# Half of a chunk's first product in Strassen's seven-product form, the second product in two PSUM banks, float16 in place of bfloat16

## The chip, the cores and the metric

One core of a Trainium2 chip. The metric is the device time of one execution, in microseconds (us). The kernel before takes 274.28 us (median of three runs, 274.2 to 274.58).

In the profile PE is TensorE's matmuls, PEld its weight loads, DVE is VectorE, ACT ScalarE, POOL GpSimd, SP SyncE.

## The reference, cut to what matters

```python
# q, k, v: 8 batches, 8 heads, 576 rows, 64 columns; w_in 512 x 2048, w_out 2048 x 512
q_s = softmax of q over its 64 columns;  k_s = softmax of k over its 576 rows
x   = q_s @ (k_s^T @ v)          # per head; put together: 4608 tokens x 512
h   = x @ w_in                   # the first product:  4608 x 512 x 2048
g   = h / (1 + exp(-h))          # Silu
out = g @ w_out                  # the second product: 4608 x 2048 x 512
```

The matmuls of `h` and `out` are nearly all the work. (The first three lines are shortened to words; the reference has them as numpy.)

## The kernel before

The tokens go in nine chunks of 512 (numbered 0 to 8; chunks 0 and 1 are special, the change concerns 2 to 8). While TensorE computes the first product of chunk t it also computes the second product of chunk t-1, in small units of four or eight matmuls (0.87 us each) that alternate. The second product is already in the seven-product (Strassen-Winograd) form: seven products of half-size blocks in place of eight, paid with sums of blocks (S1 to S4 of the activations, T1 to T4 of the weights) on VectorE.

A plain block of the first product is four matmuls into one PSUM bank, a tanh on ScalarE that reads the bank, and a "finishing product" on VectorE, `(tanh + 1) * h`, that reads the bank again. Only after it may the bank be written again. (`silu(h) = h/2 * (1 + tanh(h/2))`; tanh shares its table with exp: the trace has one table load in all.) Cuts are marked by dots, and the comments are added here.

```python
def silu(t, fb, i, o, w):                                   # i is the PSUM bank
    ...
    nc.scalar.activation(out=s, in_=i, func=ACT.Tanh, scale=OS)
    nc.vector.scalar_tensor_tensor(out=o, in0=s, scalar=1.0, in1=i, op0=ALU.add, op1=ALU.mult)

hb = [0, 2]                                                 # set to [2, 3] later: three banks rotate

def mm1(t, fb):
    bank = hb[0] % hb[1]
    hb[0] += 1
    mm1_mm(t, fb, bank, range(NC))                          # four matmuls of 512 columns
    mm1_silu(t, fb, bank)
...
WBANK = {1: 3, 6: 3, 7: 3, 4: 3, 5: 4, 3: 4, 2: 5}          # second product: three banks
...
for t in range(2, NCH):                                     # the order of units in a chunk
    begin[t] = len(units)
    bs = b_units(t - 1, ORDER)                              # 7 products x 2 halves of chunk t-1
    as_ = a_units(t)                                        # 16 plain blocks of chunk t
    plan(begin[t] + 2, lambda t=t: (s_op(t - 1, 1)))        # the sums S1 .. S4, on VectorE
    plan(begin[t] + 4, lambda t=t: (s_op(t - 1, 2)))
    plan(begin[t] + 10, lambda t=t: (s_op(t - 1, 3)))
    plan(begin[t] + 15, lambda t=t: (s_op(t - 1, 4)))
    ...                                                     # a, a, b, a, b, a, b ... one by one
...
for t in range(2, NCH - 1):                                 # attention work of batch b = t + 1
    ...                                                     # exp of q at units 4, 6; its row sums one unit later;
                                                            # exp of k at 9, 12; kv at 20; x of chunk t+1 at 25, 27
```

Each engine does its instructions in the order in which the program issues them; `plan(u, ...)` issues something just before unit u. The attention work in the last loop exists in chunks 2 to 6 (batches 3 to 7).

The softmax here doesn't subtract the row's maximum and nothing guards it: scores larger than these inputs give would overflow.

## Time and profile before

| | |
|---|---|
| time, span of the profiled run | 274.28 us, 272.5 us |
| TensorE busy | 263.6 us, 97% of the span |
| one chunk of the steady part (147.65 to 175.42 us) | 27.77 us: PE 27.56, DVE 22.16, ACT 17.31 |
| TensorE's clock | 1.00 throughout |

The page's first two parts, cut to TensorE. The rows of part 2 have one digit for each fortieth of the span: PE's busy tenths, and the clock that was granted, in tenths.

```profile
span 272.5 us, 5771 instructions
## 1 busy us (share of the span) xinstructions
PE 263.6 (97%) x2343; PEld 168.4 (62%) x2372; DVE 199.2 (73%) x290; ACT 158.2 (58%) x237; POOL 71.1 (26%) x62
## 2 busy tenths in 40 slices
PE   8999999999999999999999999999999999999993
...
PEclk9999999999999999999999999999999999999999
...
```

TensorE is the bound; nothing else is near it. The table of stretches for one chunk, us busy (with the number of instructions) for each engine, then the clock:

```profile
...
core 0: us, PE busy (x) PEld busy (x) DVE busy (x) ACT busy (x) POOL busy (x), PEclk, DMA share, GB/s
...
147.65:175.42 27.77, 27.56 (x261) 17.93 (x264) 22.16 (x31) 17.31 (x26) 7.42 (x4) 1.00 0.66 183
...
```

The longest waits of TensorE for a finishing product (engine, line, awaited; us in total, times, longest):

```profile
...
engine line waited for: us in total, times, longest us
...
PE PS L272 <- DVE GT L245: 0.3, 1, 0.3
...
```

0.3 us here, and two waits of 0.2 us in the special first chunks (another line): the three rotating banks absorb whatever VectorE is late. How late that is, the timeline of the same chunk shows (start, duration, instruction):

```profile
...
start us, us, engine line op out<-in xcount [idle before <-releaser]
...
150.08 1.03 PE L272 MATMUL PS<-XT,W 128*128 128x512 bf16 x4
...
151.15 0.60 ACT L244 ACTIVATE sg<-PS 128x512 f32<-128x512 f32 x1 [1.14 <-PE PS L272]
...
151.78 0.69 DVE L245 SCALAR_TENSOR_TENSOR GT<-sg,PS 128x512 f16<-128x512 f32 x1
...
158.38 2.29 DVE L335 TENSOR_TENSOR S<-GT 128x2048 f16<-128x2048 f16 x1
...
```

A block's matmuls run from 150.08 (ends are modelled; the next matmuls start at 150.95), its tanh starts at 151.15, its finishing product at 151.78, and its bank is free at 152.47. So an undisturbed block holds its bank for 1.5 us after its last matmul. S3 (158.38) takes 2.29 us beside GpSimd's work, where S1, a sum of the same size (at 150.64), took 1.22.

### The profile page before, as it was taken

The numbers are of one execution on the slowest core, as the hardware profiler recorded it, in microseconds if no ns is written. First come the engines' busy times: TensorE is split into PE (matmuls) and PEld (weight loads), VectorE is DVE, ScalarE is ACT, GpSimd is POOL, SyncE is SP. The second block draws the span as 40 slices with busy tenths as digits, with TensorE's granted clock in tenths as the row PEclk, the third lists the DMA queues.
The fourth block names the chain that finished last, engine by engine and source line by source line (L and its number), as shares of the span: only waits on it lengthen the run. The fifth ranks groups of instructions, "written<-read, shape, count | busy, mean of one in ns | idle before, by whom it ended". The sixth has DMA issues, their size and how long they took to land.

```text
span 272.5 us, 5771 instructions
## 1 busy us (share of the span) xinstructions
PE 263.6 (97%) x2343; PEld 168.4 (62%) x2372; DVE 199.2 (73%) x290; ACT 158.2 (58%) x237; POOL 71.1 (26%) x62
## 2 busy tenths in 40 slices
PE   8999999999999999999999999999999999999993
PEld 2467654445665566666666666666656665666783
DVE  2866765978998599749974998499837663877643
ACT  4767937667855585568546854685464446444410
POOL 1744970910470037002800180019000000000003
PEclk9999999999999999999999999999999999999999
DMA  7999999599886586648773968333134003300444
GB/s 251 321 198 352 254 339 329 169 291 377 272 169 236 112 259 144 250 98 241 170 259 81 242 176 264 81 77 67 23 69 88 2 0 77 79 0 0 95 101 116
DMA packets 35498, 45.85 MB, mean 168 GB/s; under 512 B 16208, under 2 KB 20048, under 8 KB 35472
## 3 DMA queue, kind: packets, MB, share of 16 engines
q1 hardware_dynamic: 29568, 33.69, 44.5%
q0 software_dynamic: 5584, 11.54, 16.3%
q8 instruction: 18, 0.29, 0.5%
q10 hardware_dynamic: 320, 0.26, 0.3%
q14 instruction: 8, 0.07, 0.1%
HBM read 36.70 MB, written 9.44 MB: 169 GB/s over the span
## 4 chain that ended last, share of the span: by engine, by line
PE 83%; DVE 8%; DMA 4%; ACT 2%; issue 1%; SPq 1%; POOL 1%; POOLq 0%
PE PS L272 36%; PE PS L361 33%; PE PS L301 5%; PE PS L252 4%; DMA vt<-in_v_dram 4%; DVE GT L245 2%; DVE S L335 2%; PE PS L222 2%; PE PS L183 2%; DVE zq L142 1%; SPq L95 1%; ACT sg L244 1%; DVE T L345 1%; DVE W L345 1%; POOL t L120 0%
## 5 line engine op out<-in xcount | busy, mean ns | idle before, releaser
L245 DVE SCALAR_TENSOR_TENSOR GT<-sg,PS 128x512 f16<-128x512 f32 (+2 forms) x144 | 96.3, 679 | 52.8 <-ACT sg L244 52.4
L244 ACT ACTIVATE sg<-PS 128x512 f32<-128x512 f32 (+2 forms) x144 | 85.8, 598 | 80.9 <-PE PS L272 74.1
L272 PE MATMUL PS<-XT,W 128*128 128x512 bf16 (+1 forms) x484 | 123.9, 375 | 1.8 <-DVE GT L245 0.3
L272 PEld LDWEIGHTS <-W 128*128 128x128 bf16 x512 | 49.8, 98 | 39.4 <-issue 2.1
L361 PEld LDWEIGHTS <-S 128*128 128x128 f16 x512 | 49.2, 98 | 16.6 <-issue 1.2
L151 POOL TENSOR_TENSOR eq<-eq,rzq 128x1152 bf16<-128x1152 bf16 x13 | 27.4, 2118 | 105.0 <-ACT sg L244 97.1
L361 PEld LDWEIGHTS <-GT 128*128 128x128 f16 x384 | 37.1, 98 | 13.1 <-issue 1.2
L361 PE MATMUL PS<-W,S 128*128 128x256 f16 x256 | 33.0, 273 | 0.1
L361 PE MATMUL PS<-W,GT 128*128 128x256 f16 x256 | 32.7, 273 | 0.1
L361 PE MATMUL PS<-T,S 128*128 128x256 f16 x256 | 32.7, 273 | 0.0
L335 DVE TENSOR_TENSOR S<-GT 128x2048 f16<-128x2048 f16 (+1 forms) x17 | 25.0, 1470 | 0.0
L585 POOL DMA_DIRECT2D out_dram<-ow x4 | 2.2, 552 | 75.7 <-DVE ow L570 75.7
L89 POOL CAST vaug<-vt 128x1152 bf16<-128x1152 f32 x12 | 20.4, 1732 | 0.0
L106 ACT ACTIVATE eq<-qt 128x1152 bf16<-128x1152 f32 x16 | 18.6, 1165 | 2.7 <-DMA qt<-in_q_dram 2.7
L109 ACT ACTIVATE ek<-kt 128x1152 bf16<-128x1152 f32 x16 | 18.6, 1165 | 1.3 <-DMA kt<-in_k_dram 1.3
L87 ACT CAST XT<-PS 128x1024 bf16<-128x1024 f32 (+2 forms) x18 | 17.3, 960 | 3.6 <-PE PS L222 3.6
L142 DVE TENSOR_REDUCE zq<-eq 128x18 f32<-128x1152 bf16 x12 | 16.1, 1343 | 3.8 <-ACT eq L106 3.8
L252 PE MATMUL PS<-XT,W 128*128 128x288 bf16 x128 | 16.5, 286 | 0.7 <-DVE GT L245 0.4
L361 PE MATMUL PS<-T,GT 128*128 128x256 f16 x128 | 16.5, 273 | 0.0
L301 PE MATMUL PS<-W,GT 128*128 128x512 f16 x64 | 15.6, 379 | 0.0
L252 PEld LDWEIGHTS <-W 128*128 128x128 bf16 x128 | 12.4, 98 | 4.7 <-issue 1.7
L335 DVE TENSOR_TENSOR S<-GT,S 128x2048 f16<-128x2048 f16 x8 | 13.1, 1643 | 0.0
(58 smaller groups left out, 155.7 us busy)
## 6 DMA issues: line engine op xcount, KB each, us to landing
out_dram<-ow SPq DMA_DIRECT2D x64, 128.0 KB, 2.4
qt<-in_q_dram SPq DMA_DIRECT2D x12, 576.0 KB, 5.7
kt<-in_k_dram SPq DMA_DIRECT2D x12, 576.0 KB, 7.0
vt<-in_v_dram SPq DMA_DIRECT2D x12, 576.0 KB, 7.7
qt<-in_q_dram POOLq DMA_DIRECT2D x4, 576.0 KB, 13.3
kt<-in_k_dram POOLq DMA_DIRECT2D x4, 576.0 KB, 13.7
vt<-in_v_dram POOLq DMA_DIRECT2D x4, 576.0 KB, 13.6
W<-in_moe_w_out_dram POOLq DMA_DIRECT2D x4, 512.0 KB, 15.2
```

The costliest lines, as they stand in the source:

```text
L89: eng.tensor_copy(o, i)
L106: nc.scalar.activation(out=half(st[b]["eq"], cc), in_=jgd(b, "qt", cc), func=ACT.Exp)
L109: nc.scalar.activation(out=half(ek, cc), in_=jgd(b, "kt", cc), func=ACT.Exp)
L142: nc.vector.reduce_sum(out=z, in_=e, axis=AX.X)
L151: eng.tensor_tensor(out=e, in0=e, in1=r[:, :, :, None].to_broadcast([128, J, 2, D]), op=ALU.mult)
L244: nc.scalar.activation(out=s, in_=i, func=ACT.Tanh, scale=OS)
L245: nc.vector.scalar_tensor_tensor(out=o, in0=s, scalar=1.0, in1=i, op0=ALU.add, op1=ALU.mult)
L252: nc.tensor.matmul(out=PS[:, 2 * (fb % 3) + n, 0:S // 2], lhsT=W1[:, c, fb * 128:(fb + 1) * 128], rhs=XTS[0][:, c, n * (S // 2):(n + 1) * ...
L272: nc.tensor.matmul(out=PS[:, bank, o0:TCH], lhsT=W1[:, c, fb * 128:(fb + 1) * 128], rhs=XTS[t % 2][:, c, o0:TCH], start=(c == 0), stop=(c ...
L301: nc.tensor.matmul(out=PS[:, 2 + tb, :], lhsT=GTS[t % 2][:, fc, tb * 128:(tb + 1) * 128], rhs=W2[:, fc, :], start=(fc == 0), stop=(fc == N ...
L335: nc.vector.tensor_tensor(out=SS[i - 1][:, f], in0=in0[:, f], in1=in1[:, f], op=op)
L361: nc.tensor.matmul(out=PS[:, bank, m * HN:(m + 1) * HN], lhsT=a[:, fc, m * 128:(m + 1) * 128], rhs=bb[:, fc, :], start=(first and fc == 0) ...
```

## The change

It puts half of the first product of chunks 2 to 8 into the seven-product form too: of 16 hidden tiles, eight stay plain blocks, and eight are done by seven products ("groups") of eight 256-column matmuls each, 56 matmuls of 256 columns in place of 32 of 512. The sums are eight small tensor operations: four of the weights, once, and four of x (XS1 to XS4), per chunk; the results are joined from PSUM by three copies and Silus on ScalarE and three adds on VectorE. To have four banks (0 to 3) for this, the second product is squeezed from three banks into two. Smaller things: float16 in place of bfloat16 for x and the first weights, x scaled by 0.5 (by 8 before), two load buffers in place of three and one of exp of q in place of two, S3 written in place, the last output copy on VectorE, kv and x of the attention work moved by one or two units.

The core of the diff, with cuts marked (the comments are added here):

```diff
-    XS = 8.0
+    XS = 0.5
...
+    def group_snap(i):                       # ScalarE: PSUM banks 0,1 to SBUF
+        H[i] = mp.tile([128, 2 * TCH], FP32, name=f"h{i}", bufs=1)
+        nc.scalar.copy(out=H[i], in_=PS[:, 0:2, :].rearrange("p b n -> p (b n)"))
+    def group_add(i):                        # VectorE: banks 2,3 + H
+        nc.vector.tensor_tensor(
+            out=H[i], in0=PS[:, 2:4, :].rearrange("p b n -> p (b n)"), in1=H[i], op=ALU.add
+        )
+    def group_silu(t, i, f, n):
+        x = group_bank(0) if i is None else four(H[i])
+        nc.scalar.activation(out=group_out(t, f, n), in_=x, func=ACT.Silu, scale=1.0 / XS)
+    def group(t, i):
+        bank = 0 if i in (1, 6, 7, 4) else 2
...
+        for p in range(4):
+            for c in range(2):
+                nc.tensor.matmul(
+                    out=PS[:, bank + p // 2, (p % 2) * HT:(p % 2 + 1) * HT],
+                    lhsT=a[:, c, p * 128:(p + 1) * 128],
+                    rhs=bb[:, c, :],
...
-    WBANK = {1: 3, 6: 3, 7: 3, 4: 3, 5: 4, 3: 4, 2: 5}
+    WBANK = {1: 4, 6: 4, 7: 4, 4: 4, 5: 5, 3: 5, 2: 5}
...
-    ORDER = (1, 5, 6, 2, 7, 4, 3)
+    ORDER = (1, 2, 6, 5, 7, 4, 3)
...
+        ps_ = [lambda t=t, fb=fb: mm1(t, fb) for fb in (0, 8, 1, 9, 2, 10, 3, 11)]
+        gs = [lambda t=t, i=i: group(t, i) for i in (1, 2, 6, 5, 7, 4, 3)]
+        plan(begin[t] + 2, lambda t=t: s_op(t - 1, 1))
+        plan(begin[t] + 4, lambda t=t: s_op(t - 1, 2))
+        plan(begin[t] + 11, lambda t=t: s_op(t - 1, 3))
+        plan(begin[t] + 16, lambda t=t: s_op(t - 1, 4))
+        mix = "pbpbpbpbpbpbpbp", "ggbgbgbgbbgbgb"     # p plain block, b second product, g group
+        for x in "".join(mix) if t < NCH - 1 else "ggbgbgbgbbgbgb" + "pbpbpbpbpbpbpbp":
+            units.append({"p": ps_, "b": bs, "g": gs}[x].pop(0))
+        x = begin[t] + 9 if t < NCH - 1 else begin[t]
+        plan(x, lambda t=t: (xs_op(t, 1), xs_op(t, 2), xs_op(t, 3), xs_op(t, 4)))
...
+    plan(begin[2], lambda: (hb.__setitem__(0, 1), hb.__setitem__(1, 4)))   # banks 1,2,3,0,1,...
```

More of the change, by code (lines that the diff above doesn't have):

```diff
@@ L51 @@
     glob = ctx.enter_context(tc.tile_pool(name="glob", bufs=1))
-    ld = ctx.enter_context(tc.tile_pool(name="ld", bufs=3))
+    ld = ctx.enter_context(tc.tile_pool(name="ld", bufs=2))
     ap = ctx.enter_context(tc.tile_pool(name="ap", bufs=1))
@@ L55 @@
     ps = ctx.enter_context(tc.tile_pool(name="ps", bufs=1, space=bass.MemoryType.PSUM))
-    W1 = glob.tile([128, NC, DFF], BF16, name="W1")
+    W1 = glob.tile([128, NC, DFF], FP16, name="W1")
     W2 = glob.tile([128, NFB, DM], FP16, name="W2")
@@ L62 @@
     GTS = [glob.tile([128, NFB, S], FP16, name="GT0"), glob.tile([128, NFB, TCH], FP16, name="GT1")]
-    SS = [glob.tile([128, HF, HT], FP16, name=f"S{i + 1}") for i in range(4)]
-    XTS = [glob.tile([128, NC, S], BF16, name=f"XT{i}") for i in range(2)]
+    SS = {i: glob.tile([128, HF, HT], FP16, name=f"S{i}") for i in (1, 2, 4)}
+    WS = [glob.tile([128, 2, 512], FP16, name=f"WS{i + 1}") for i in range(4)]
+    XS4 = [glob.tile([128, 2, HT], FP16, name=f"XS{i + 1}") for i in range(4)]
+    XTS = [glob.tile([128, NC, S], FP16, name=f"XT{i}") for i in range(2)]
     vaug = glob.tile([128, J, NG, E1], BF16, name="vaug")
@@ L104, in exp_q @@
         if "eq" not in st[b]:
-            st[b]["eq"] = ap.tile([128, J, NG * D], BF16, name="eq", bufs=2)
+            st[b]["eq"] = ap.tile([128, J, NG * D], BF16, name="eq")
         nc.scalar.activation(out=half(st[b]["eq"], cc), in_=jgd(b, "qt", cc), func=ACT.Exp)
@@ L288, in mm1, with wa, xb, ws_op @@
         mm1_silu(t, fb, bank)
+    F0, F1 = 12, 4
+    H = [None] * 3
+    def wa(c, f):
+        return W1[:, 2 * c:2 * c + 2, f * 128:(f + 4) * 128]
+    def xb(t, c, n):
+        return XTS[t % 2][:, 2 * c:2 * c + 2, (1 - n) * HT:(2 - n) * HT]
+    def ws_op(i):
+        in0, in1, op = {
+            1: (wa(0, F1), wa(1, F1), ALU.add),
+            2: (WS[0], wa(0, F0), ALU.subtract),
+            3: (wa(0, F0), wa(0, F1), ALU.subtract),
+            4: (wa(1, F0), WS[1], ALU.subtract),
+        }[i]
+        nc.vector.tensor_tensor(out=WS[i - 1], in0=in0, in1=in1, op=op)
@@ new lines, in xs_op, with group_out, four, group_bank @@
+    def xs_op(t, i):
+        in0, in1 = {
+            1: (xb(t, 0, 1), xb(t, 0, 0)),
+            2: (xb(t, 1, 1), XS4[0]),
+            3: (xb(t, 1, 1), xb(t, 0, 1)),
+            4: (xb(t, 1, 0), XS4[1]),
+        }[i]
+        nc.vector.tensor_tensor(out=XS4[i - 1], in0=in0, in1=in1, op=ALU.subtract)
+    def group_out(t, f, n):
+        return GTS[t % 2][:, f:f + 4, (1 - n) * HT:(2 - n) * HT]
+    def four(x):
+        return x.rearrange("p (f n) -> p f n", f=4)
+    def group_bank(bank):
+        return PS[:, bank:bank + 2, :].rearrange("p b (f n) -> p (b f) n", f=2)
@@ new lines, in group @@
+    def group(t, i):
+        bank = 0 if i in (1, 6, 7, 4) else 2
+        a, bb = {
+            1: (wa(0, F0), xb(t, 0, 0)),
+            2: (wa(1, F0), xb(t, 1, 0)),
+            3: (WS[3], xb(t, 1, 1)),
+            4: (wa(1, F1), XS4[3]),
+            5: (WS[0], XS4[0]),
+            6: (WS[1], XS4[1]),
+            7: (WS[2], XS4[2]),
+        }[i]
+        for p in range(4):
[4 more added lines that the diff above has]
+                    rhs=bb[:, c, :],
+                    start=(i in (1, 2, 5) and c == 0 and p % 2 == 0),
+                    stop=(i in (2, 3, 4) and c == 1 and p % 2 == 1),
+                    skip_group_check=True,
+                )
+        if i == 1:
+            group_snap(0)
+        elif i == 2:
+            group_add(0)
+        elif i == 6:
+            group_snap(1)
+            group_silu(t, 0, F0, 0)
+        elif i == 7:
+            group_snap(2)
+            group_add(2)
+        elif i == 4:
+            group_silu(t, None, F1, 0)
+        elif i == 3:
+            group_silu(t, 2, F1, 1)
+            group_add(1)
+            group_silu(t, 1, F0, 1)
@@ L329, in s_op @@
             1: (blk(t, 0, 1), blk(t, 1, 1), ALU.add),
-            2: (SS[0], blk(t, 0, 0), ALU.subtract),
+            2: (SS[1], blk(t, 0, 0), ALU.subtract),
             3: (blk(t, 0, 0), blk(t, 0, 1), ALU.subtract),
-            4: (blk(t, 1, 0), SS[1], ALU.subtract),
+            4: (blk(t, 1, 0), SS[2], ALU.subtract),
         }[i]
         f = slice(f0, f1)
-        nc.vector.tensor_tensor(out=SS[i - 1][:, f], in0=in0[:, f], in1=in1[:, f], op=op)
+        o = blk(t, 0, 1) if i == 3 else SS[i]
+        nc.vector.tensor_tensor(out=o[:, f], in0=in0[:, f], in1=in1[:, f], op=op)
     def t_op(i, eng, f0=0, f1=HF):
@@ L351, in prod @@
             2: (blk(t, 1, 0), B21),
-            3: (SS[3], B22),
+            3: (SS[4], B22),
             4: (blk(t, 1, 1), T4),
-            5: (SS[0], T1),
-            6: (SS[1], T2),
-            7: (SS[2], T3),
+            5: (SS[1], T1),
+            6: (SS[2], T2),
+            7: (blk(t, 0, 1), T3),
         }[i]
@@ L373, in w_out_tile, with snap @@
         return WG[t]["o", m]
-    def snap(t, name):
+    def snap(t, name, bank=4):
         WG[t][name] = mp.tile([128, 512], FP32, name=name, bufs=1)
-        nc.scalar.activation(out=WG[t][name], in_=PS[:, 3, :], func=ACT.Copy, scale=OS)
+        nc.scalar.activation(out=WG[t][name], in_=PS[:, bank, :], func=ACT.Copy, scale=OS)
     def w_add(t, name, bank, m, n):
@@ L391, in w_last @@
         o = w_out_tile(t, 1)[:, :, 0:HN]
-        nc.scalar.activation(
-            out=o, in_=PS[:, 3, :].rearrange("p (a n) -> p a n", a=2), func=ACT.Copy, scale=OS
+        nc.vector.tensor_scalar_mul(
+            out=o, in0=PS[:, 4, :].rearrange("p (a n) -> p a n", a=2), scalar1=OS
         )
@@ L409, in after @@
             snap(t, "sc")
-            w_add(t, "sc", 4, 1, 1)
+            w_add(t, "sc", 5, 1, 1)
         elif i == 4:
@@ L414, in after @@
         elif i == 3:
-            w_add(t, "sb", 4, 0, 1)
+            w_add(t, "sb", 5, 0, 1)
             w_store(t, 0)
@@ L543 @@
         bs = b_units(t - 1, ORDER)
-        as_ = a_units(t)
-        plan(begin[t] + 2, lambda t=t: (s_op(t - 1, 1)))
-        plan(begin[t] + 4, lambda t=t: (s_op(t - 1, 2)))
-        plan(begin[t] + 10, lambda t=t: (s_op(t - 1, 3)))
-        plan(begin[t] + 15, lambda t=t: (s_op(t - 1, 4)))
-        seq = as_[:1]
-        as_ = as_[1:]
-        for i, x in enumerate(bs):
-            if as_:
-                seq.append(as_.pop(0))
-            if i == 10 and as_:
-                seq.append(as_.pop(0))
-            seq.append(x)
-        seq += as_
-        units += seq
+        ps_ = [lambda t=t, fb=fb: mm1(t, fb) for fb in (0, 8, 1, 9, 2, 10, 3, 11)]
[7 more added lines that the diff above has]
+            units.append({"p": ps_, "b": bs, "g": gs}[x].pop(0))
+        assert not (ps_ or bs or gs)
+        x = begin[t] + 9 if t < NCH - 1 else begin[t]
+        plan(x, lambda t=t: (xs_op(t, 1), xs_op(t, 2), xs_op(t, 3), xs_op(t, 4)))
     begin[NCH] = len(units)
     last = NCH - 1
-    plan(begin[NCH] - 9, lambda: s_op(last, 1, 0, 4))
-    plan(begin[NCH] - 7, lambda: s_op(last, 2, 0, 4))
-    plan(begin[NCH], lambda: (s_op(last, 1, 4, 8), s_op(last, 2, 4, 8), s_op(last, 3)))
+    plan(begin[NCH] - 9, lambda: s_op(last, 1, 4, 8))
+    plan(begin[NCH] - 7, lambda: s_op(last, 2, 4, 8))
+    plan(begin[NCH], lambda: (s_op(last, 1, 0, 4), s_op(last, 2, 0, 4), s_op(last, 3)))
     plan(begin[NCH] + 6, lambda: s_op(last, 4))
@@ L595, in end @@
         else:
-            prod(last, i, m)
+            prod(last, i, m, bank=5 if i == 2 else 3)
         if i == 3:
@@ L599, in end @@
         elif m == 1 and i in (1, 6, 7):
-            snap(last, {1: "sa", 6: "sb", 7: "sc"}[i])
+            snap(last, {1: "sa", 6: "sb", 7: "sc"}[i], 3)
         if m == 1 and i == 2:
@@ L632 @@
     plan(b1, lambda: (load(2, "kt", k, 0, nc.gpsimd), load(2, "kt", k, 1, nc.gpsimd)))
-    plan(b1, lambda: (load(2, "vt", v, 0, nc.gpsimd), load(2, "vt", v, 1, nc.gpsimd)))
     plan(b1, lambda: nc.gpsimd.tensor_copy(GTS[1][:, :, 0:64], GTS[0][:, :, TCH:S]))
+    plan(b1 + 6, lambda: (load(2, "vt", v, 0, nc.gpsimd), load(2, "vt", v, 1, nc.gpsimd)))
     plan(b1 + 4, lambda: vcast(1, 0, nc.scalar))
@@ L641 @@
     plan(b1 + 9, lambda: xt(1, 1))
+    plan(b1 + 3, lambda: (ws_op(1), ws_op(2)))
+    plan(b1 + 9, lambda: (ws_op(3), ws_op(4)))
     plan(b1 + 8, lambda: t_op(1, nc.vector, 0, 4))
@@ L684 @@
                     pl(x + 6, lambda i=i, b=b: load(b + 1, "vt", v, i, nc.sync))
-            pl(20, lambda b=b: kv_both(b))
-        for i, x in enumerate((25, 27)):
-            pl(x, lambda i=i, t=t: xt(t + 1, i))
+            plan(u + 22, lambda b=b: kv_both(b))
+        for i, x in enumerate((24, 27)):
+            plan(u + x, lambda i=i, t=t: xt(t + 1, i))
     for u, f in enumerate(units):
```

## The prediction

> **What bounds it now.** TensorE: 97% busy on the page; the chain of waits runs almost only over PE (first-product matmuls 36%, second-product 33%). In the table of windows a chunk takes 27.78 us with PE busy 27.57, VectorE 22.2, ScalarE 17.3. VectorE is not spare early in a chunk: the timeline shows it solid from 150.6 to 166.3 us. The finishing product follows its matmuls by up to 3 us without stopping PE, because three banks rotate.
>
> **What PE saves.** Four 512-column matmuls take 0.862 us start to start, eight of 256 columns 0.868. Half the first product was 32 x 0.2155 = 6.90 us per chunk; it becomes 56 x 0.1085 = 6.08. Seven chunks: 5.8 us. Weight loads (98 ns) stay hidden, as in the second product.
>
> **What the others get, per chunk.** ScalarE: 8 tanh fewer (-4.8), three 128x1024 copies and four Silus (about 1.0 each, as the 128x1024 eviction of x) +7, last copy moved away -0.6. Exp and Silu should also switch the table twice. The Trainium skill (ScalarE: Activation LUTs, "What ACT_TABLE_LOAD costs") says 1283 ns a load, as the trace's one load took; I assume Silu is not in exp's set. VectorE: 8 finishing products fewer (-5.5), three 128x1024 adds +3.6 (estimate from 0.69 at 512), four x sums +1.7 (estimate from 0.68 at 1024, 1.22 at 2048; nearly double beside GpSimd, as S3's 2.29 shows), last copy +0.7. By its sum neither becomes the bound.
>
> **Where it goes wrong: order.** A chunk is now eight plain first-product blocks alternating with second-product halves (13 us of PE), then the seven products. Plain blocks rotate over banks 1, 2, 3, 0; the eighth writes bank 0, and the very next unit, product 1, writes bank 0. PE must wait for that block's tanh and finishing product. Undisturbed that is 1.5 us (150.95 to 152.47 in the timeline): over six chunks (the last starts with the products) +9, more than is gained. And VectorE is disturbed: up to the eighth finishing product it has, in order, eight of them (4.8), S1, S2 (2.3), two row sums (3.2), an output add (0.6), four x sums (2.6 beside GpSimd), S3 (2.3): nearly 16 us, plus some 3 us of waiting for tanh behind exp and table load. It is done near 19 us into the chunk; PE wants bank 0 at 13. Estimated stall: 6 us in chunks 3 to 6, 7 in chunk 2 (T3, T4 too), 1.6 in chunk 7. About 1 us of it comes earlier, where product 5 waits for its bank.
>
> Sum: 274.3 - 5.8 + 24 + 7 + 1.6, less a little: about 300 us.  Idle of 5 us may also lower PE's clock (Trainium skill, TensorE: Matmul & The Clock Gate, "The HAM clock gate": an idle window of about 3.4 us halves it; no run here shows it), costing more.
>
> **Prediction: 300 us, 280 to 312. Faster by over 2%: 0.06; within 2%: 0.10; slower: 0.84.**
>
> **What would show it.** One long PE idle per chunk before product 1 in chunks 2 to 7, ended by the finishing product; ScalarE idle then, VectorE full; chunk period about 33 us; two table loads in chunks 3 to 6; PE matmul time down about 5.8 us; chunk 8 shorter than before.
>
> **What would make it wrong.** VectorE keeping pace early (the 1.5 us floor: near 278), or an order I misread (269).

## The result, and the profile after

The kernel after takes 318.26 us (median of four, 317.32 to 318.82) against 274.25: ratio 1.160, 95% interval 1.157 to 1.163. Ratios are the mean time of one kernel's runs over that of the other's of the same rounds, so they are not quite the ratio of the medians quoted. The direction and the cause were foreseen; the size, 300 us with a top of 312, was not.

The page, cut as before:

```profile
span 316.8 us, 6096 instructions
## 1 busy us (share of the span) xinstructions
PE 271.6 (86%) x2539; PEld 190.5 (60%) x2540; DVE 211.2 (67%) x294; ACT 182.4 (58%) x232; POOL 67.5 (21%) x62
## 2 busy tenths in 40 slices
PE   8799999988299955998299974999379989999994
...
PEclk9999999999679997999879997899979999999999
...
```

TensorE's idle time (span less busy) rose from 8.9 to 45.2 us, by 36.3. Its busy time rose by 8.0 as well, although it has less to multiply: the PEclk row shows why, with 6, 7, 8 where it was 9 throughout. There are five such dips, one in each of chunks 2 to 6. One chunk, with the columns as before:

```profile
...
core 0: us, PE busy (x) PEld busy (x) DVE busy (x) ACT busy (x) POOL busy (x), PEclk, DMA share, GB/s
137.20:173.80 36.60, 29.73 (x290) 21.60 (x289) 23.57 (x31) 21.76 (x28) 6.82 (x4) 0.91 0.52 143
...
```

36.6 us in place of 27.8, at a mean clock of 0.91. The waits of TensorE:

```profile
...
engine line waited for: us in total, times, longest us
PE PS L357 <- DVE GT L247: 32.0, 6, 7.2
PE PS L455 <- DVE ow L475: 3.7, 4, 0.9
...
```

Six waits for a finishing product, 32.0 us, before products 1 of chunks 2 to 7, and four short ones of the second product. The timeline of the chunk:

```profile
...
start us, us, engine line op out<-in xcount [idle before <-releaser]
...
142.19 1.28 ACT L108 ACT_TABLE_LOAD   x1
...
150.73 1.40 DVE L320 TENSOR_TENSOR XS<-XT 128x512 f16<-128x512 f16 x1
...
152.16 1.26 DVE L320 TENSOR_TENSOR XS<-XT,XS 128x512 f16<-128x512 f16 x1
152.20 0.60 ACT L246 ACTIVATE sg<-PS 128x512 f32<-128x512 f32 x1 [1.47 <-PE PS L274]
153.34 1.37 DVE L320 TENSOR_TENSOR XS<-XT 128x512 f16<-128x512 f16 x1
...
155.56 1.21 DVE L429 TENSOR_TENSOR GT<-GT 128x2048 f16<-128x2048 f16 x1
...
156.70 1.27 DVE L247 SCALAR_TENSOR_TENSOR GT<-sg,PS 128x512 f16<-128x512 f32 x2
...
158.03 3.57 PE L357 MATMUL PS<-XT,W 128*128 128x256 f16 x16 [5.86 <-DVE GT L247]
...
```

The eighth block's tanh (152.20) is done at 152.8. VectorE is then in the x sums (150.73 to 155.04; each 1.3 to 1.4 us until GpSimd ends at 154.4, the last only 0.41), and does the sixth finishing product, S3, and at last the seventh and eighth (156.70, x2, until 157.97). At 158.03 TensorE starts products 1 and 2, after 5.86 us of idling. The sixteen matmuls then take 3.57 us; in run 1 below the same sixteen take 1.91 at full clock. The same stretch by the us, columns as before (the clock is the 1.00 or 0.50 ahead of the last two numbers):

```profile
...
155.00:156.00 1.00, 0.00 (x0) 0.00 (x0) 1.00 (x3) 0.00 (x0) 0.00 (x0) 1.00 1.00 195
156.00:157.00 1.00, 0.00 (x0) 0.00 (x0) 1.00 (x2) 0.00 (x0) 0.00 (x0) 0.50 0.52 35
...
158.00:159.00 1.00, 0.97 (x5) 0.71 (x5) 1.00 (x1) 0.00 (x0) 0.00 (x0) 0.50 1.03 389
...
161.00:162.00 1.00, 1.00 (x6) 0.72 (x5) 0.29 (x1) 0.00 (x0) 0.00 (x0) 0.50 0.69 267
...
```

The clock is 1.00 until 156, four us after TensorE stopped, and then 0.50. It is still 0.50 at 161 to 162 and 0.59 in the us after that: nearly five us of work after the wait (158.03 to about 162.8) run at half speed, which costs about 2.4 us. This differs by chunk: the work done at half clock in chunks 2 to 6 is 5.8, 2.9, 4.8, 5.8 and 2.9 us, 22.1 in all, which costs about 11 us (half of it; an estimate, since PE's ends are modelled).

### The profile page after: what moved, and what is told of

The parts are those of the page before. It is cut to its first block, busy times and chain, and to the rows that moved or that the text cites. A ratio compares the mean times of both kernels' runs of the same rounds, so it can differ in the third digit from the quotient of the medians.

```text
span 316.8 us, 6096 instructions
## 1 busy us (share of the span) xinstructions
PE 271.6 (86%) x2539; PEld 190.5 (60%) x2540; DVE 211.2 (67%) x294; ACT 182.4 (58%) x232; POOL 67.5 (21%) x62
## 4 chain that ended last, share of the span: by engine, by line
PE 49%; DVE 30%; ACT 12%; issue 4%; DMA 3%; SPq 1%; POOL 1%; DVEq 0%; ACTq 0%
PE PS L455 17%; PE PS L357 14%; DVE GT L247 9%; PE PS L274 7%; DVE XS L320 7%; PE PS L393 4%; DVE zq L144 4%; PE PS L254 3%; DMA vt<-in_v_dram 3%; ACT sg L246 3%; ACT GT L342 2%; DVE ow L475 2%; ACT L342 2%; DVE GT L429 2%; PE PS L224 2%
## 5 line engine op out<-in xcount | busy, mean ns | idle before, releaser
L247 DVE SCALAR_TENSOR_TENSOR GT<-sg,PS 128x512 f16<-128x512 f32 (+2 forms) x88 | 58.8, 678 | 29.1 <-ACT sg L246 28.7
L274 PE MATMUL PS<-XT,W 128*128 128x512 f16 (+1 forms) x288 | 71.3, 373 | 1.1 <-DVE GT L247 0.8
L246 ACT ACTIVATE sg<-PS 128x512 f32<-128x512 f32 (+2 forms) x88 | 51.7, 597 | 34.0 <-PE PS L274 29.6
L333 ACT COPY h<-PS 128x1024 f32<-128x1024 f32 x21 | 21.2, 1011 | 59.8 <-PE PS L357 59.8
L357 PE MATMUL PS<-XT,W 128*128 128x256 f16 x112 | 21.1, 369 | 32.0 <-DVE GT L247 32.0
L336 DVE TENSOR_TENSOR h<-PS,h 128x1024 f32<-128x1024 f32 x21 | 25.7, 1225 | 30.9 <-PE PS L357 26.4
L357 PEld LDWEIGHTS <-W 128*128 128x128 f16 x168 | 20.0, 119 | 39.8 <-issue 33.7
L274 PEld LDWEIGHTS <-W 128*128 128x128 f16 x288 | 27.9, 98 | 22.3 <-issue 2.4
L357 PEld LDWEIGHTS <-WS 128*128 128x128 f16 x224 | 21.5, 100 | 4.3 <-issue 1.2
L342 ACT ACTIVATE GT<-h 128x1024 f16<-128x1024 f32 x21 | 22.2, 1058 | 2.1 <-DVE h L336 2.1
L357 PE MATMUL PS<-XS,WS 128*128 128x256 f16 x168 | 22.5, 279 | 0.0
```

The costliest lines, as they stand in the source:

```text
L274: nc.tensor.matmul(out=PS[:, bank, o0:TCH], lhsT=W1[:, c, fb * 128:(fb + 1) * 128], rhs=XTS[t % 2][:, c, o0:TCH], start=(c == 0), stop=(c ...
L333: nc.scalar.copy(out=H[i], in_=PS[:, 0:2, :].rearrange("p b n -> p (b n)"))
L336: nc.vector.tensor_tensor(out=H[i], in0=PS[:, 2:4, :].rearrange("p b n -> p (b n)"), in1=H[i], op=ALU.add)
L342: nc.scalar.activation(out=group_out(t, f, n), in_=x, func=ACT.Silu, scale=1.0 / XS)
L357: nc.tensor.matmul(out=PS[:, bank + p // 2, (p % 2) * HT:(p % 2 + 1) * HT], lhsT=a[:, c, p * 128:(p + 1) * 128], rhs=bb[:, c, :], start=(i ...
```

## The experiments

The theory (A): VectorE is behind when the eighth plain block has to leave bank 0, because the chunk's first part now holds nearly all of VectorE's in-order work and product 1, the next unit, needs bank 0; and the idle time lowers TensorE's clock. Rivals: (B) the activation table switches cause the lag; (C) the products themselves are slow, by their operands or banks, or the seven-product form has a cost of its own; (D) the side parts of the change (two banks, fewer buffers, float16) cost the time.

### 1. Dummy matmuls in the wait (`a_heat`)

```diff
         gs = [lambda t=t, i=i: group(t, i) for i in (1, 2, 6, 5, 7, 4, 3)]
+        if t < NCH - 2:
+            gs[0] = lambda t=t: (heat(18, 6), group(t, 1))
```

> Only edit: in chunks 2 to 6, eighteen dummy 512-column matmuls (3.9 us at full clock) into the free bank 6 just before product 1, where the trace shows TensorE idle for 5.86 us (7.19 in chunk 2). Work is added, nothing is taken away. Theory A (idle lets the clock fall to 0.50, and the 16 matmuls of products 1 and 2 then take 3.3 to 3.6 us instead of 1.9): the stall stays 5.9 us, the clock stays 1.0, and the kernel gets FASTER by 1.7 to 2.2 us in each of five chunks: about 308 us. Rival (products 1 and 2 are slow for their own sake, by bank or operand): unchanged, 318 us, or slower by the dummies.

309.88 us (307.45 to 311.74), ratio 1.131 where the change alone has 1.160. Adding 18 matmuls a chunk made the kernel about 8 us faster. The profiled run has clock 0.999, and products 1 and 2 take 1.91 us:

```profile
...
153.43 1.91 PE L357 MATMUL PS<-XT,W 128*128 128x256 f16 x16 [1.97 <-DVE GT L247]
...
```

So the products are not slow for their own sake (C falls for this part), and the clock's share is real. How large it is, this profiled run shows best: its span is 305.7 us against 316.8, 11.1 less, and each of its chunks 3 to 6 takes 34.24 us, where those of the change alone take 35.6 to 37.1. Runs of this kernel with a clock of 0.986 and 0.994 took 311.7 and 309.8 us, the one with 0.999 took 307.5: even the filled gap is not always safe.

### 2. The x sums first (`b_xs_early`)

```diff
-        x = begin[t] + 9 if t < NCH - 1 else begin[t]
+        x = begin[t]
```

> Only edit: the four x sums are issued at the first unit of the chunk instead of the tenth, so VectorE does them before GpSimd's work begins. Theory A (the stall is VectorE's lag at the eighth finishing product, and the x sums beside GpSimd, 4.2 us of it, are the largest removable part): the sums fall to about 0.42 us each, the stall in chunks 2 to 6 goes from 5.9 to between 1.5 and 2.5 us, the clock stays at 1.0: 318 - 5 x 3.8 - 10 = about 289 us. Rival B (the activation table switch causes the lag): the sums only change places, over 308 us.

293.23 us (290.92 to 294.23), ratio 1.067: 25 us of the 44 gone with one line. The x sums take 0.42 us each, before GpSimd starts, and S3 took 1.60 in their place beside it:

```profile
...
131.15 0.42 DVE L320 TENSOR_TENSOR XS<-XT,XS 128x512 f16<-128x512 f16 x1
...
142.99 1.60 DVE L429 TENSOR_TENSOR GT<-GT 128x2048 f16<-128x2048 f16 x1
...
```

The wait of chunks 3 to 7 fell to 2.0 us or less (4.65 in chunk 2, where T3 and T4 still stand in front). The result is 4 us above the expectation, and two lines show where part of it went:

```profile
...
115.45 1.91 PE L357 MATMUL PS<-XT,W 128*128 128x256 f16 x16 [2.00 <-DVE GT L247]
...
145.84 3.38 PE L357 MATMUL PS<-XT,W 128*128 128x256 f16 x16 [2.01 <-DVE GT L247]
...
```

The same wait of 2.0 us before products 1 and 2, in chunks 3 and 4: once the products take 1.91 us, once 3.38, at a clock of 0.50. (In this profiled run work at half clock costs about 2.9 us in chunk 2 and 1.7 in chunk 4.) The 0.92 us wait for the output add before it is not the difference, since chunks 3 to 6 all have it. The difference is where the wait falls. In the twelve profiled runs the clock changes only at whole multiples of 3.41 us after its first change (the half-clock stretches of the kernel after last 10.24, 3.41, 6.83, 6.83 and 3.41 us), and the waits do not shift these points. Between two of them TensorE was idle for 1.90 us in chunk 3 and for 2.01 us in chunk 4 (length less PE's busy time; columns as before):

```profile
...
111.93:115.34 3.41, 1.51 (x10) 0.82 (x9) 3.41 (x6) 0.66 (x2) 3.41 (x3) 1.00 0.66 198
115.34:118.75 3.41, 3.30 (x31) 2.96 (x31) 3.23 (x3) 1.02 (x1) 0.98 (x1) 1.00 0.96 201
...
142.65:146.06 3.41, 1.40 (x10) 0.72 (x9) 3.41 (x5) 0.60 (x1) 3.41 (x3) 1.00 0.66 173
146.06:149.47 3.41, 3.41 (x19) 2.35 (x17) 1.86 (x2) 1.01 (x1) 0.64 (x1) 0.50 0.95 203
...
```

Over all twelve traces, at full clock, the clock fell after every such stretch with 2.01 us of idle time or more, and after none with 1.98 or less. So a wait of 2 us costs nothing more or 1.7 us more, by where it happens to fall.

### 3. Another bank for the eighth block (`c_hb0`)

```diff
-    plan(begin[2], lambda: (hb.__setitem__(0, 1), hb.__setitem__(1, 4)))
+    plan(begin[2], lambda: (hb.__setitem__(0, 0), hb.__setitem__(1, 4)))
```

> Only edit: the plain blocks rotate over banks 0,1,2,3 instead of 1,2,3,0, so the eighth block ends in bank 3 and product 1 needs the banks of the fifth and sixth, product 2 those of the seventh and eighth. Theory A: first half of product 1 starts without a wait, second half waits for the sixth finishing product, product 2 still for the eighth, so VectorE's lag is nearly all still paid (about 1 us per chunk regained), but the idle time is cut in two pieces[...] and the clock may hold: 302 us if it holds, 309 if not. If the shared bank 0 alone were the cause (VectorE on time), about 280.

308.09 us (307.9 to 309.14), ratio 1.123. The wait is cut in two, and the clock fell all the same (0.967 over the run): the two waits fall into one stretch of 3.41 us, 2.79 us of them in chunk 4. TensorE's lines in chunk 4:

```profile
...
151.30 0.60 PE L357 MATMUL PS<-XT,W 128*128 128x256 f16 x4 [3.09 <-DVE GT L247]
153.04 1.87 PE L357 MATMUL PS<-XT,W 128*128 128x256 f16 x8 [1.14 <-DVE GT L247]
...
```

Four matmuls of product 1 after 3.09 us of waiting, then the eight of product 2 after 1.14 more, in 1.87 us where eight take 1.04 at full clock. 4.23 us of waiting in place of 5.86. The collision of one bank is thus only the place where the lag is paid. Moved by one bank, it is paid one product later.

### 4. No table switch (`d_tanh`)

```diff
-        nc.scalar.activation(out=group_out(t, f, n), in_=x, func=ACT.Silu, scale=1.0 / XS)
+        nc.scalar.activation(out=group_out(t, f, n), in_=x, func=ACT.Tanh, scale=1.0 / XS)
```

> Only edit: Silu becomes Tanh, a wrong result on purpose, so that no activation table is switched (nine loads fewer, same sizes). Theory A: exp starts 1.3 us earlier in chunks 3 to 6, the stall there goes from 5.9 to about 4.6 us, still long enough for the clock to fall: about 312 us. Rival B (the table switch causes the lag): stall near 1.5 us and about 288 us.

The result is wrong on purpose (relative error 0.60). 310.02 us (308.85 to 310.86), ratio 1.129: 8 us, where A expected 6, and not the 30 of rival B. The waits:

```profile
...
PE PS L357 <- DVE GT L247: 30.7, 6, 7.2
...
```

The single wait before product 1 only fell from 5.86 to 5.52 us in chunks 3 to 6, which looks like a miss against the 4.6 expected. But the wait of 0.9 us for product 5 before it is gone altogether; the two together fell by 0.92 + 5.86 - 5.52 = 1.26 us, the 1.28 of one table load. By the profiled spans (316.8 and 309.1), 5.1 us of the gain is idle time and 2.6 busy time; of the latter 1.6 is less work at half clock (18.9 us of it in place of 22.1, an estimate).

### 5. Banks 6 and 7 for the last two blocks (`e_banks`)

```diff
         bank = hb[0] % hb[1]
+        if hb[1] == 8:
+            bank = (0, 1, 2, 3, 0, 1, 6, 7)[bank]
...
-    plan(begin[2], lambda: (hb.__setitem__(0, 1), hb.__setitem__(1, 4)))
+    plan(begin[2], lambda: (hb.__setitem__(0, 0), hb.__setitem__(1, 8)))
```

> Only edit: the eight plain blocks of a chunk use banks 0,1,2,3,0,1,6,7 (6 and 7 are idle in that part of the chunk), so that product 1 needs the banks of the fifth and sixth block and product 2 those of the third and fourth; VectorE's work keeps its order. Theory A (lag times shared bank): the wait before product 1 shrinks from 5.9 to about 3 us (its second half waits for the sixth finishing product behind the x sums), the clock stays at 1.0; about 295 us. If the lag did not matter and only the collision of bank 0 did, the whole wait goes: about 285 us or less. If the clock still falls: about 303.

298.42 us (297.74 to 300.05), ratio 1.087. The wait before product 1's second half is 3.09 us in chunks 3 to 6, as expected, and the clock still fell in some of them (mean 0.976), which the expectation of 295 us had not counted.

### 6. Banks and early x sums together (`f_banks_xs`)

The edits of 2 and 5.

> The bank order of the run with other banks and the early x sums together. Theory A: the wait at product 1 is gone in chunks 3 to 7; what remains is 0.9 us where product 5 waits for the output add behind the row sums, about 1 us where its bank waits for the first add of product 2 behind S3 and S4, and some 3 us in chunk 2: about 280 us. A rival (the seven-product form costs more by itself, on ScalarE or by weight loads, than the wait shows) would leave it above 286.

281.7 us (281.61 to 281.86), ratio 1.027, clock 0.994. No wait before product 1 is left. The list of waits names what remains:

```profile
...
PE PS L359 <- DVE h L338: 6.7, 5, 3.6
PE PS L457 <- DVE ow L477: 3.7, 4, 0.9
...
```

Product 5 of the groups waits for the first add of product 2 (`h`, behind S3 and S4 in VectorE's order; 3.6 us in chunk 2, 0.77 in chunks 3 to 6), product 5 of the second product for the output add behind the row sums (0.92 in each of four chunks). Each is an order on VectorE.

### 7. The side parts alone (`h_plain`)

The kernel after with all 16 blocks plain, interleaved as before, and without the group sums:

```diff
-        for x in "".join(mix) if t < NCH - 1 else "ggbgbgbgbbgbgb" + "pbpbpbpbpbpbpbp":
-            units.append({"p": ps_, "b": bs, "g": gs}[x].pop(0))
...
+        as_ = a_units(t)
+        ...                      # a, a, b, a, b, ... as in the kernel before, S1..S4 at 2, 4, 10, 15
...
-    plan(b1 + 3, lambda: (ws_op(1), ws_op(2)))
-    plan(b1 + 9, lambda: (ws_op(3), ws_op(4)))
```

> The other half of the change alone: float16 x and weights, x halved, second product in two banks in the order 1,2,6,5,7,4,3, fewer load buffers, S3 in place, the last copy on VectorE; but the first product all in plain blocks, interleaved as before, without its sums. Theory A: none of this costs time: 274.3 us within 1.5 us. Rival (two banks or fewer buffers stall): over 278 us.

275.54 us (275.3 to 275.77) against 274.33, ratio 1.004 (1.003 to 1.005). Rival D falls. The 1.2 us is small but real; the trace has two waits of TensorE that before doesn't have, 0.8 us for a finishing product where chunk 2 begins and 0.4 us for the copy of kv. (A third, 1.3 us at the very start, costs nothing: the matmul behind it starts at 8.69, and before at 8.64.) Which of the side parts makes them was not tried. The steady chunk takes 27.78 us, as before.

### 8. S3, S4, T3 and T4 later (`i_all`)

On top of 6:

```diff
-        plan(begin[t] + 11, lambda t=t: s_op(t - 1, 3))
-        plan(begin[t] + 16, lambda t=t: s_op(t - 1, 4))
+        plan(begin[t] + 16, lambda t=t: s_op(t - 1, 3))
+        plan(begin[t] + 20, lambda t=t: s_op(t - 1, 4))
...
-    plan(begin[2] + 12, lambda: t_op(3, nc.vector))
-    plan(begin[2] + 14, lambda: t_op(4, nc.vector, 0, 4))
-    plan(begin[2] + 16, lambda: t_op(4, nc.vector, 4, 8))
+    plan(begin[2] + 17, lambda: t_op(3, nc.vector))
+    plan(begin[2] + 19, lambda: t_op(4, nc.vector, 0, 4))
+    plan(begin[2] + 21, lambda: t_op(4, nc.vector, 4, 8))
...
-                pl(x + 1, lambda i=i, b=b: (qsum(b, i), qnorm(b, i, nc.gpsimd)))
+                pl(x + 1 + i, lambda i=i, b=b: (qsum(b, i), qnorm(b, i, nc.gpsimd)))
```

> As the run with banks and early x sums, with S3 and S4 (and T3, T4 in chunk 2) issued in the second part of the chunk, and the second row sum behind the output add. Theory A: VectorE is ahead of TensorE in the first part, neither of the two small waits is left, a chunk takes 26.9 to 27.3 us: 268.5 (the 5.8 us of matmul time saved, all of it) to 273 us, faster than before. If over 275, another wait exists that I have not named.

273.83 us (273.13 to 274.03) against 274.33, ratio 0.998 (0.996 to 0.999): level with before, and short of the 273 at the top of the expectation. Its list of waits has 1.3 us for T3 in chunk 2 and 1.3 us for S3 in chunk 8, and its timeline 0.3 us a chunk before product 5, behind an S3 of 2.18 us beside GpSimd.

### 9. S3 still later (`j_late_s3`)

```diff
-        plan(begin[t] + 16, lambda t=t: s_op(t - 1, 3))
-        plan(begin[t] + 20, lambda t=t: s_op(t - 1, 4))
+        plan(begin[t] + (17 if t < NCH - 1 else 11), lambda t=t: s_op(t - 1, 3))
+        plan(begin[t] + (20 if t < NCH - 1 else 16), lambda t=t: s_op(t - 1, 4))
...
-    plan(begin[2] + 17, lambda: t_op(3, nc.vector))
+    plan(begin[2] + 13, lambda: t_op(3, nc.vector))
```

> The version that came out best (banks, early x sums, late S3, S4, T3, T4), with three orders mended where its trace still shows TensorE waiting: S3 behind the first add of product 2 (0.3 us a chunk in chunks 3 to 6), T3 earlier in chunk 2 (1.3 us), and S3, S4 of the last chunk at their first places (1.3 us). Theory A: the waits go and with them 3 us: about 270.5 us, against 274.3 before. If it stays at 273.8, those waits were not on the chain.

276.61 us (276.1 to 276.92), ratio 1.006: a miss, and in the wrong direction. The waits in chunks 2 and 8 that it aimed at went, but S3, now behind an add that itself waits for ScalarE's copy, came too late for product 7 in six chunks:

```profile
...
PE PS L457 <- DVE GT L431: 6.8, 6, 1.2
...
```

That I had not checked when issuing it: the add waits, and what stands behind it in the same engine's order waits too.

### 10. S3 early (`k_early_s3`)

```diff
-        plan(begin[t] + (17 if t < NCH - 1 else 11), lambda t=t: s_op(t - 1, 3))
+        plan(begin[t] + (4 if t < NCH - 1 else 11), lambda t=t: s_op(t - 1, 3))
```

> The run before, with S3 issued right behind S2 in chunks 2 to 7 (into the 1.1 us in which VectorE idles behind exp and the table load, and before GpSimd starts, so 1.2 us instead of 2.2) rather than behind the add of product 2, where TensorE waited 1.18 us for it in five chunks and about 0.9 in another. Theory A (what is left are single waits for VectorE's order): 276.6 - 6.8 = about 270 us, faster than before by 1.5%. Rival (the seven-product form has a cost of its own of some 3 to 4 us that the order can't remove): not below 273.

269.72 us (268.94 to 270.69) against 274.65, ratio 0.982 (0.980 to 0.985): the version that beats both kernels, with correct results. Its page and one chunk:

```profile
span 267.6 us, 6100 instructions
## 1 busy us (share of the span) xinstructions
PE 259.4 (97%) x2539; PEld 185.1 (69%) x2540; DVE 197.8 (74%) x294; ACT 182.4 (68%) x232; POOL 66.4 (25%) x62
...
```

```profile
...
core 0: us, PE busy (x) PEld busy (x) DVE busy (x) ACT busy (x) POOL busy (x), PEclk, DMA share, GB/s
118.12:145.28 27.16, 27.07 (x290) 20.38 (x288) 20.90 (x31) 21.73 (x27) 6.44 (x4) 1.00 0.73 194
...
```

27.16 us a chunk, clock 1.00, and the list of waits has none of TensorE in chunks 2 to 8. Against the side parts alone (1.004 to 0.982, two ratios to the same kernel before) the seven-product form is worth 2.2% of 274.5, 5.9 us, of which 1.2 are the two waits of run 7, which this version doesn't have. A steady chunk shows less than the 0.83 us that the prediction had costed: 27.78 to 27.16, 0.62 us, about 4.3 in seven chunks (an estimate). So the form has no large cost of its own that an order can't hide, and the rest of rival C falls too; where the missing 0.2 us a chunk goes was not tried.

## Why the prediction was wrong

Point by point.

- *TensorE bounds the kernel, and 5.8 us of matmul time is saved.* Right in kind, somewhat less in size: 0.62 us a chunk, about 4.3 (run 10).
- *Neither ScalarE nor VectorE becomes the bound by its sum.* Right. After the change DVE is busy 211.2 of 316.8 us, and run 10 has the same work in 269.7 us.
- *The eighth block leaves bank 0 too late for product 1.* Right: six waits, before products 1 of chunks 2 to 7, ended by the finishing product.
- *How long:* 6 us in chunks 3 to 6 was foreseen (of which about 1 for product 5), 7 in chunk 2, 1.6 in chunk 7. Measured: 5.86 and 0.92, 7.19, 1.41. In sum 32.6 foreseen, 32.0 + 3.7 = 35.7 measured: 3 us of the miss.
- *Its parts:* the x sums were estimated at 2.6 us beside GpSimd, "nearly double"; they took 4.3, single ones 1.37 where 0.42 is undisturbed. S3 was put at 2.3 and took 1.21, since GpSimd was done by then. The two errors nearly cancel.
- *Two table loads in chunks 3 to 6, Silu not in exp's set.* Right: nine loads of 1283 ns in chunks 2 to 6, before Silu and before exp. Run 4 shows their worth, 8 us.
- *"Idle of 5 us may also lower PE's clock ... costing more."* This is the step that failed. The mechanism was named and then left out of the sum: it was entered with 0 us, and it cost about 11. Half of the work at half clock is 11 us (above), and the run of experiment 1 whose clock held, without any work removed, is 11.1 us shorter. As a check, the same matmuls keep TensorE busy for 271.6 us in the kernel after and for 259.4 in run 10, where the clock is 0.996: 12.2 us, an estimate, since ends of matmuls are modelled.

With that term the sum is 274.3 - 5.8 + 35.7 + 11 = 315.2, 3 us under the 318.3 measured; the smaller saving of matmul time is about 1.5 of them, and a wait of 0.8 us where chunk 2 begins, which run 7 has too, another part. The prediction without the term ends at 301 before the deduction "a little less", and 300 after. That deduction had no base either: nothing was regained in the waits.

The Trainium skill (TensorE: Matmul & The Clock Gate, "Part 1: The HAM clock gate") had what the sum needed: half clock after an idle window of about 3.4 us, and full clock only after about 3.4 us of work. An estimate from that page alone would have been 3.4 / 2 = 1.7 us for each of five chunks, 8.5 us, a figure that belonged into the sum. This trace agrees on the size of the drop (0.50) and on the length of the window: the slow stretches last one to three times 3.41 us. But the work that they hold is not always 3.4 us: 2.9 us in chunks 3 and 6, 4.8 in chunk 4, 5.8 in chunks 2 and 5, so that the cost is 1.4 to 2.9 us a chunk, and 11 in all.

## What to carry to other kernels

When work moves between engines, add up the in-order queue of the helping engine up to the first place where the bounding engine must wait for it, not over the whole chunk: a chunk with 20% of slack on VectorE lost 6 us because nearly all of VectorE's work came before one bank's release. When waits of 2 us or more on TensorE are foreseen, enter the slow clock after them as a term of the sum (here 1.4 to 2.9 us each). And a regression of 16% was an order: the same products, chiefly with the x sums and S3 put into VectorE's idle time and the last two blocks into banks that were free, ran 1.8% faster than before.

## What the Trainium skill lacked or had wrong

- TensorE: Matmul & The Clock Gate, its advice on idle gaps (none over about 3 us), was too lax here. In run 2 the clock fell to 0.50 after a wait of 2.01 us in one chunk, and stayed at 1.00 after waits of the same length in three others. The page says that the window is free-running, and asks for an idle window; here 2.01 us of idle time within a stretch of 3.41 us was enough, and 1.98 was not. In run 3 parts of two waits (3.09 and 1.14 us) added up to 2.79 in one stretch.
- ScalarE: Activation LUTs, "What ACT_TABLE_LOAD costs", gives 2.66 us for a switch, with a drain. Here a switch in a running stream cost the load alone: the copy before it ends at 142.17, the load runs from 142.19 for 1.28 us, exp starts at 143.48; and run 4 gained 1.26 us per load on the chain. The page's table of sets doesn't list Silu: the trace has loads before Silu and before exp, and none for the tanh that follows Silu.
- GPSIMD Engine Reference, "1. Specifications", says that GpSimd's SBUF interfaces are shared with VectorE, with no size of it. Here float16 sums of two SBUF inputs went from 0.42 to 1.37 us (128x512, beside GpSimd's multiplications and casts), and from 1.22 to 2.29 us (128x2048, S3 of the kernel before). The size is not missing from the skill, though: SBUF — State Buffer, "SBUF: two separate sides", says that of such an instruction and a GpSimd instruction that reads SBUF the one that starts first blocks the other until it ends. The trace fits that: the three slow x sums of chunk 4 end at 152.13, 153.42 and 154.71, each 0.3 us after a GpSimd instruction ends (151.85, 153.14, 154.44). So a short sum loses what is left of GpSimd's instruction, not a share of its own time.
